# A new order of all steps, with the loads split and dealt anew to two queues, in a linear-attention and FFN kernel

## The chip, the cores and the metric

The kernel runs on one core of a Trainium2 chip. A core has five engines with an instruction queue each: TensorE (PE in the profile, with its weight loads as PEld), VectorE (DVE), ScalarE (ACT), GpSimd (POOL) and SyncE (SP). Each works through its queue in order. DMAs are issued by SP and ACT here, and moved by 16 DMA engines that both queues share. The metric is the device time of one execution in microseconds (us).

## The reference

Two branches read the same layer-normalized input, and the result is added to x. There is one batch of S = 2048 rows, width D = 448, H = 16 heads of 28, and F = 1792.

```python
xn = _layernorm(x)                                # no scale, no bias
# A: linear attention with a softmax feature map
q, k, v = split_heads(xn @ wqkv)
pq, pk = q @ w_phi, k @ w_phi                     # per head, 28 x 28
phi = lambda p: concat([softmax(p), softmax(-p)]) # 56 features a head
kv, z = phi(pk).T @ v, phi(pk).sum(rows)
o = (phi(pq) @ kv) / (phi(pq) @ z + 1e-6)
A = o @ wo
# B: FFN with Mish
h = xn @ w1 + b1
B = (h * tanh(softplus(h))) @ w2
return x + A + B
```

## The kernel before, in words

**An order written out by hand.** All work is cut into named steps. `ORDER` (L147) is a string of their names, and `run_order` calls them one after the other. Each step appends its instructions to the queues of the engines that it uses, and `Program.op` notes what each instruction reads and writes. `resolve` turns that into semaphore waits. So the string alone sets the order on each engine, and what waits for what follows from the data. Matmuls, evacuations and transposes go through helpers, so many steps share a line: L429 (`run`) issues the products of q, k, v and the first FFN layer, L509 and L511 (`evac`) copy PSUM to SBUF on ACT and DVE.

**Names of steps.** u is a pair of row tiles (0 to 7), t one tile (0 to 15). A final letter a, d, p, s or m names the engine (ACT, DVE, POOL, SP) or, for m, a DMA transpose issued by SP; b is a PE transpose evacuated by both ACT and DVE.

- `lx a.b`: load of x tiles a to b-1. `lkm`, `lvm`: rows 0 to 383 of the K and V weights; `lkt`: rows 384 to 447 of both, into each half of the partitions. `lp`: the 28 x 28 phi matrices in four small DMAs. `lqT0` to `lqT3`: the q weights by DMA transpose into `WqT`. `lb`: b1. `l1m`, `l1t`: W1's main and tail rows, `l2`: W2, `lo`: Wo.
- `pi`, `pw`, `pv`, `pp`, `pk`, `zero`: POOL writes constants (identity, zeros of Wbd, ones beside v, pads, mask, zeros for the products of `z`).
- `st t`: mean and variance of a tile (DVE: `BATCH_NORM_STATS2` at L466; ACT: two passes with a sum, L458 and L462). `rt`, `rs`: the reciprocal standard deviation of one or two tiles. `xn t`: normalize a tile; on ACT and POOL this first needs a shift that DVE computes (L486). `xt u`: transpose a normalized pair into `xnT`.
- `z12`: 12 products of zeros (L370). `wtk h`: PE transposes of the K weights into `WT`; `wmk h` and `wmq h`: fold phi into the K and Q weights (L571), results in `Wp[1]` (Wpk) and `Wp[0]` (Wpq). `qd` (DVE, L289) doubles columns of `WqT` and reads all four of its loads. `b1`: transpose of the bias.
- `k`, `q`, `v` with u and a part, `f q.fc` with a part: products of 64 weight rows at a time, which run in pairs on the two halves of the array. Parts A and B hold six matmuls each, H two (the tail rows). When the last part of a step is issued, its evacuation follows: two exponentials on ACT for k and q (L609, L682), one copy for v, one Mish on ACT for f (L703).
- `kn u.s`, `kc u`: normalize phi of the keys: sum and reciprocal on DVE, product on POOL (L621, L633). `kv u`: accumulate phi(k)ᵀv (L650), eight steps into one pair of banks; `kvz` evacuates it and SP transposes it into `KVZ`.
- `e t`: DMA transpose of phi(q) of a tile. `nd t`: numerator and denominator of a tile (PE at L723, then seven DVE instructions). `ot u`: transpose of the result. `wo u` with a part (L845) and `g t` (L828): the output projection and the second FFN layer, which accumulate into one bank per tile; the last of the four adds x on DVE (L793). `sto`, `stt`: stores.

**What sets the waits.** PSUM has eight banks, used as four pairs. `take2` gives a step the pair that has been idle longest in the order; a step's first product waits until that pair's last evacuation is done. A part of a step waits for the data named in its list `r`, before the change for all rows of its weight, tails included.

Of the kernel before, what the change touches and what calls it, by code (L numbers as in the profile page):

```python
# [5 lines left out]
ACT = mybir.ActivationFunctionType  # L6
# [6 lines left out]
D = 448  # L13
H = 16
# [136 lines left out]
st13d xn6d l1ts st15d xn7d xt3m v0Ha wmq1a wmq0a k2A rt12p rt13p xn13p xn12p st10d xt6m xn8p st14d k1A v1Bd k1B st11d  # L151
q2B k1H rs5p v1Ad q1H q2H v1Hd rt14a q1B xn10d q2A xn9d xn14d rt15p pk xt4m q0A q1A q0B k3B xn15d xt7m v6Ba k3H q0H
v6Aa xn11p kn0.1 k6H v6Ha k3A kn0.0 xt5m kn1.1 l1ms k6A v3Ad kc3 k6B v3Hd k7A v3Bd k7H v4Hd kn6.0 e3 v4Ad k7B v4Bd k4B
v7Ba k4H k4A e2 k5B kn7.1 v7Aa kn7.0 q4H k5A v7Ha kc2 e0 k5H q4A e5 f0.0B q4B f0.0H v5Bd f0.0A e9 f0.8H f0.8A v5Ad
kn5.0 f0.3B f0.8B v5Hd f0.3A e1 f0.4B f0.3H e8 q3B f0.4A f0.5A f0.4H f0.5H f0.2H f0.2A kn1.0 f0.5B kn4.1 q5H e4 q5A
f0.2B q3H kn6.1 loa q7B q5B q7A q7H kn5.1 kn4.0 kv2 kv6 ep kv1 kv0 kv5 kv7 kv4 kv3 q3A f1.0B kvz f0.9A e10 f1.0A f1.0H
e14 f0.9H e15 f0.6A f0.9B f0.7B f0.6H nd0 f0.7A f0.6B f0.11H f0.11A f0.7H f0.10B nd3 f0.11B f0.12A f0.10A e11 e6
f0.10H nd1 f0.12H e7 ot0m f0.1B f0.12B f0.1A f0.1H q6A q6H f1.13H nd2 q6B f1.5A f1.13A f1.4A f1.13B f1.5H f1.1H f1.1A
f1.4B f1.1B f1.5B f1.6A f1.6H e12 f1.4H ot1m f1.11A f1.6B f1.11B nd4 f1.12H f1.11H l2s f1.12A f0.13B f1.12B f1.7A nd5
f1.7H f0.13H f0.13A f1.2H f1.7B ot2m f1.2A nd7 wo0H f1.2B wo1B wo0A wo1A nd6 ot3m wo1H wo0B nd10 g2 g7 g3 g1 g0 nd12  # L160
e13 f1.10A f1.10H f1.9A f1.9H wo3B f1.10B nd13 f1.9B wo3A wo3H f1.8B ot6m f1.3H nd11 f1.3A ot5m g6 g5 f1.8H nd15 f1.8A
wo2H f1.3B sto1 wo2B nd14 nd9 wo2A nd8 g4 sto3 g14 g9 sto2 g12 ot7m g8 ot4m g13 wo7H wo4B wo7A wo5A wo6A wo5H wo6H
wo4A wob wo5B wo4H wo6B wo7B sto0 g10 g11 g15 sto6 stt14 sto5 sto4 stt15
"""
# [7 lines left out]
def _kernel(es, nc, A_x, A_wqkv, A_w_phi, A_wo, B_w1, B_b1, B_w2, out):  # L172
# [421 lines left out]

    def tok_works(u, W):
        return lambda b: [(bank(b + par)[:, 0:D],
                           lambda c, k, par=par: xnT[k[0]:k[1], u, xchunk(c, par), :],
                           lambda c, k: W[k[0]:k[1], c, :]) for par in range(2)]

    def v_mm(u, part, eng):  # L600
# [3 lines left out]
        pair_part(f"v{u}", part, tok_works(u, Wv), [("xnT", u), ("xnU", u)] + rows_of("Wv"), then)  # L604

    def k_mm(u, part):
        def then(b):
            for s in range(2):
                op("ACT", lambda e, s=s: e.activation(E_of(u)[:, s, :, :], two(b, D), ACT.Exp,  # L609
                                                      scale=1.0 if s == 0 else -1.0),  # L610
                   r=[pb(b), pb(b + 1)], w=[("E", u, s)], tag=f"exk{u}.{s}")
        pair_part(f"k{u}", part, tok_works(u, Wp[1]), [("xnT", u), ("xnU", u)] + [("Wp", 1, h, c) for h in range(2) for c in range(2)], then)

# [78 lines left out]

# [6 lines left out]
    def ffn1(q, fc, part):  # L699
        def then(b):  # L700
# [99 lines left out]
    def last_columns(t, b):  # L800
# [3 lines left out]
        def f(e):  # L804
# [6 lines left out]
            return ins  # L811
        pe(f, [("WoB",), ("W2",), ("oT", t // 2)] + [("act", fc, t // 8) for fc in range(FC)] + [("Wo", n) for n in range(4)],
           [pb(b)], f"l{t}")
# [166 lines left out]
```

## Time and profile before

| | |
|---|---|
| median of 3 runs | 154.04 us (153.67 to 154.15) |
| the profiled execution | 153.96 us, span 152.2 us |
| PE busy | 144.6 us (95%) |
| DVE busy | 101.1 us (66%) |
| ACT busy | 75.7 us (50%) |
| POOL busy | 44.3 us (29%) |
| chain that ended last | PE 78%, ACT 12%, DMA 4%, DVE 3% |

The span runs from the first to the last instruction; the execution's own time is 1.76 us longer. Shares of busy time are averages over the whole span. The chain is followed back from the last instruction, at each step to what released it.

### The profile page before, as it was taken

The numbers are of one execution on the slowest core, as the hardware profiler recorded it, in microseconds if no ns is written. First come the engines' busy times: TensorE is split into PE (matmuls) and PEld (weight loads), VectorE is DVE, ScalarE is ACT, GpSimd is POOL, SyncE is SP. The second block draws the span as 40 slices with busy tenths as digits, with TensorE's granted clock in tenths as the row PEclk, the third lists the DMA queues.
The fourth block names the chain that finished last, engine by engine and source line by source line (L and its number), as shares of the span: only waits on it lengthen the run. The fifth ranks groups of instructions, "written<-read, shape, count | busy, mean of one in ns | idle before, by whom it ended". The sixth has DMA issues, their size and how long they took to land.

```text
span 152.2 us, 3611 instructions
## 1 busy us (share of the span) xinstructions
PE 144.6 (95%) x1541; PEld 76.1 (50%) x1541; DVE 101.1 (66%) x223; ACT 75.7 (50%) x90; POOL 44.3 (29%) x65
## 2 busy tenths in 40 slices
PE   3978999989999979999999999999999999999993
PEld 1454545445444574445344455554544554559552
DVE  0699989599969903599606999535995999200721
ACT  3485999995995699778997730000500400000000
POOL 3385688969999950000000000000000000000000
PEclk9999999999999999999999999999999999999999
DMA  5995964989967243994399260500035000540204
GB/s 123 288 260 147 174 143 93 131 268 262 101 137 138 76 139 73 180 197 41 60 149 321 86 65 14 119 0 0 2 65 151 30 4 0 121 121 4 87 4 151
DMA packets 40436, 17.22 MB, mean 113 GB/s; under 512 B 34020, under 2 KB 39908, under 8 KB 40420
## 3 DMA queue, kind: packets, MB, share of 16 engines
q1 hardware_dynamic: 37548, 14.46, 46.9%
q10 hardware_dynamic: 2872, 2.53, 5.6%
q8 instruction: 12, 0.20, 0.5%
q14 instruction: 4, 0.03, 0.1%
HBM read 7.02 MB, written 1.84 MB: 58 GB/s over the span
## 4 chain that ended last, share of the span: by engine, by line
PE 78%; ACT 12%; DMA 4%; DVE 3%; issue 1%; ACTq 0%
PE PS L429 38%; PE PS L828 28%; PE PS L845 7%; DMA x_all<-in_A_x_dram 4%; ACT actT L609 3%; PE PS L723 2%; PE PS L650 2%; ACT actT L682 2%; ACT v_all L509 2%; DVE Sk L627 1%; ACT Wpq L509 1%; ACT Eq L682 1%; DVE v_all L511 1%; ACT Eq L509 1%; ACT Wpk L509 1%
## 5 line engine op out<-in xcount | busy, mean ns | idle before, releaser
L703 ACT ACTIVATE actT<-PS,b1T 128x1024 bf16<-128x1024 f32 x28 | 30.2, 1112 | 33.1 <-PE PS L429 33.0
L429 PE MATMUL PS<-xnT,W 64*128 64x512 bf16 x392 | 46.2, 376 | 0.0
L828 PE MATMUL PS<-W,actT 128*128 128x448 bf16 (+1 forms) x224 | 42.7, 351 | 0.0
L828 PEld LDWEIGHTS PS<-W,actT 128*128 128x128 bf16 x224 | 21.5, 98 | 20.3 <-issue 0.7
L429 PEld LDWEIGHTS PS<-xnT,W 64*128 64x128 bf16 x392 | 18.1, 94 | 21.0 <-ACT actT L703 0.4
L793 DVE TENSOR_TENSOR x_all<-PS,x_all 128x448 bf16<-128x448 f32 (+1 forms) x16 | 9.5, 616 | 20.3 <-PE PS L845 10.3
L621 POOL TENSOR_TENSOR actT<-actT,rSk 128x896 bf16<-128x896 bf16 x12 | 20.0, 1699 | 0.0
L609 ACT ACTIVATE actT<-PS 128x896 bf16<-128x896 f32 x16 | 13.7, 950 | 3.7 <-DVE stats L466 1.8
L429 PE MATMUL PS<-Wkv,xnT 64*128 64x448 bf16 x112 | 13.6, 349 | 0.6 <-DVE v_all L511 0.6
L429 PE MATMUL PS<-Wpk,xnT 64*128 64x448 bf16 x112 | 13.3, 349 | 0.5 <-ACT Wpk L509 0.5
L429 PE MATMUL PS<-Wpq,xnT 64*128 64x448 bf16 x112 | 12.7, 350 | 0.0
L466 DVE BATCH_NORM_STATS2 stats<-x_all 128x6 f32<-128x448 bf16 x15 | 9.2, 614 | 5.2 <-DMA x_all<-in_A_x_dram 5.2
L617 DVE TENSOR_REDUCE Sk<-actT 128x32 f32<-128x896 bf16 x12 | 12.5, 1043 | 0.0
L738 DVE COPY Sq<-PS 128x16 f32<-128x16 f32 x32 | 4.0, 167 | 12.5 <-PE PS L723 12.2
L749 DVE TENSOR_TENSOR xn<-v_all,rden 128x448 bf16<-128x448 f32 x16 | 10.0, 625 | 1.3 <-DMA Wkv<-xn 0.8
L746 DVE TENSOR_TENSOR v_all<-v_all 128x464 f32<-128x464 f32 x16 | 10.3, 642 | 0.6
L742 DVE TENSOR_TENSOR v_all<-PS,Sq 128x464 f32<-128x464 f32 x16 | 10.3, 642 | 0.5
L744 DVE TENSOR_TENSOR v_all<-PS,Sq 128x464 f32<-128x464 f32 x16 | 10.1, 630 | 0.0
L429 PEld LDWEIGHTS PS<-Wkv,xnT 64*128 64x128 bf16 x112 | 5.4, 94 | 6.0 <-DVE v_all L511 1.0
L682 ACT ACTIVATE actT<-PS 128x896 bf16<-128x896 f32 x10 | 8.4, 926 | 0.0
L429 PEld LDWEIGHTS PS<-Wpk,xnT 64*128 64x128 bf16 x112 | 5.3, 94 | 5.5 <-ACT Wpk L509 0.6
L429 PEld LDWEIGHTS PS<-Wpq,xnT 64*128 64x128 bf16 x112 | 5.1, 94 | 5.4 <-ACT actT L609 0.5
(85 smaller groups left out, 137.7 us busy)
## 6 DMA issues: line engine op xcount, KB each, us to landing
W<-in_B_w_dram SPq DMA_DIRECT2D x1, 1568.0 KB, 8.0
out_dram<-x_all SPq DMA_DIRECT2D x7, 224.0 KB, 2.2
W<-in_B_w_dram SPq DMA_DIRECT2D x1, 1344.0 KB, 7.2
x_all<-in_A_x_dram ACTq DMA_DIRECT2D x5, 224.0 KB, 4.1
Wo<-in_A_wo_dram ACTq DMA_DIRECT2D x2, 336.0 KB, 3.6
x_all<-in_A_x_dram SPq DMA_DIRECT2D x2, 224.0 KB, 4.9
W<-in_B_w_dram SPq DMA_DIRECT2D x2, 224.0 KB, 4.0
Wkv<-in_A_wqkv_dram SPq DMA_DIRECT2D x1, 336.0 KB, 4.2
```

Of the source, the lines that this page charges most:

```text
L429: ins = e.matmul(o, lhs(c, k), rhs(c, k), start=first and n == at[par][0], stop=last and n == at[par][-1])
L609: op("ACT", lambda e, s=s: e.activation(E_of(u)[:, s, :, :], two(b, D), ACT.Exp, scale=1.0 if s == 0 else -1.0), r=[pb(b), pb(b + 1)], w=[ ...
L617: op("DVE", lambda e: e.tensor_reduce(Sk[u][:, s, :], Eh(), AX.X, ALU.add), r=[("E", u, s)], w=[("Sk", u, s)], tag=f"Sk{u}.{s}")
L621: op("POOL", lambda e: e.tensor_tensor(Eh(), Eh(), ap_on(rSk[u][:, s, 0:1], [[1, 2 * H], [0, DH]]), ALU.mult), r=[("E", u, s), ("rSk", u, ...
L682: op("ACT", lambda e, s=s: e.activation(Eq_of(u)[:, :, s, :].rearrange("p i (h n) -> p i h n", n=64)[:, :, :, 0:QP], two(b, D).rearrange(" ...
L703: op("ACT", lambda e: e.activation(actT[:, q, fc, :], bank(b, 2), ACT.Mish, bias=b1T[:, fc:fc + 1]), r=[("b1T",), pb(b), pb(b + 1)], w=[(" ...
L742: op("DVE", lambda e: e.tensor_tensor(tv(t1[i]), num(0), sx(1), ALU.mult), r=[pb(b), pb(b + 1), ("Sq", i, 1)], w=[("t1", i)], tag=f"ta{t}")
L744: op("DVE", lambda e: e.tensor_tensor(tv(t2), num(1), sx(0), ALU.mult), r=[pb(b), pb(b + 1), ("Sq", i, 0)], w=[("t2",)], tag=f"tb{t}")
L746: op("DVE", lambda e: e.tensor_tensor(t1[i], t1[i], t2, ALU.add), r=[("t1", i), ("t2",)], w=[("t1", i)], tag=f"tc{t}")
L749: op("DVE", lambda e: e.tensor_tensor(o_sb[(t // 2) % 2][:, t % 2, :].rearrange("p (h d) -> p h d", d=DH), t1[i][:, :, 0:DH], ap_on(rden[i ...
L828: ins = e.matmul(bank(b)[:, 0:width(t)], act_of(fc, t), W2[:, fc, 0:width(t)], start=first and fc == 0, stop=last and fc == FC - 1)
L845: ins = e.matmul(bank(b)[:, 0:w], oT_of(u)[lo:hi, cc * P:(cc + 1) * P], Wo[lo:hi, cc, 0:w], start=first and n == at[par][0], stop=last and ...
```

## The change

The order is written anew from the first step to the last. With it:

- Loads. SP: x0-1, tail of Wv, b1, phi, Wv, x6-7, x8-11, the four WqT transposes, then x12-13 and W1's first and third part between the transposes of x. ACT: x4-5, x2-3, Wk, tail of Wk and Wv (to partitions 0 to 63 only; 64 to 127 get Wv's alone), x14-15, W1's second part. The tail of Wk is transposed from 64 rows and doubled in the evacuation (`doubled`).
- W1's main rows come in three loads, W2 in four (two issued by each of SP and ACT), Wo by SP.
- A part waits only for the rows that it reads: A and B for the main rows, H for the tails (`rows_of`, `folded`, `turned`).
- `y5.1` and `z10`: 11 products of zeros instead of 12, with `zero` ahead of `pi` on POOL.
- `wtk0` and `wtk1` are evacuated by ACT and DVE together, `wmk0` by ACT instead of DVE, `wmq1` by DVE instead of ACT. v2 and v7 go to DVE, v3, v4 and v5 to ACT. Statistics: tiles 1 and 10 on ACT, 5 on DVE.
- The first products are v0 and v2 (k0 and k2 before). The order of keys on DVE and POOL, of the f, nd and g steps, and of the stores is new too.
- Functions for early products on centred x (`center`, `center_T`, `minus_rstd`, `v_early`, `k_early`, `q_early`) are added; no step of the order calls them.

```diff
 ORDER = """
-pi lx1.2a pw table lx0.1s lx4.6a lx2.4a zero st1d lpa st5a st0d st4d st2d rs0p lvma rs2p lx6.8a xn0a xn1d lkms xn5p
-lkts xn4p lx8.10s lbs st3d z12 wtk0a rt2a wtk1d xt0b lqT3 rt3a wmk0d wmk1a pp b1 xt2b xn2d st8d lqT1 lqT2 lqT0 xn3d
-st9d k0B lx12.14a k2B xt1m st7d qd lx10.12s lx14.16a rt8p pv st6d k0A k0H st12d rt9p k2H v2Ba v0Ba v2Ha v2Aa v0Aa rs3p
...
+lx0.2s lx4.6a pw lvts zero st0d y5.1 lx2.4a pi lbs st4d pv rt4p table lkma lkta lps st1a rs0a st5d lvms xn0a rt5a xn1d
+xn4p st2d xn5p rt2a lx6.8s z10 b1 st3d xt0b rt3p wtk0b wtk1b xt2b wmk0a xn2d wmk1a lx8.12s xn3d v0Ba st6d st7d lqT0
+v2Bd st11d lqT2 v0Aa lx14.16a lqT3 st10a k2A rs3p st8d v0Ha k2H v2Hd lqT1 k0H xn6d rs5p xt1m qd v2Ad k2B k0B st9d
+wmq1d wmq0a k0A xn7d k1A k1H rt8p rt9p q0A xn9d lx12.14s pp xn8p k1B st15d xn10p q0H q1H q1A st14d st12d l1c0s q0B
+st13d xn11d xt3m v1Ad q2H q1B rs6p v1Hd xt4m pk q2A v1Bd q2B k4A v3Ba l1c2s k4H xt5m v4Ba v3Aa xn13d rs7a v3Ha k4B
+xn12d v4Aa k5H xn14d v5Ba xn15p xt6m k5B v4Ha v5Ha k5A kn1.1 k6B v6Ha v5Aa k6A v6Ba xt7m e2 e3 l1c1a kn1.0 k6H k7H
+kn4.0 k7A v7Hd kn4.1 kn2.0 kn2.1 v7Ad v6Aa k7B kc6 k3B v7Bd l1ts k3A k3H q4B f0.0B l2p0a q4H q4A f0.3A f0.0A f0.6B
+f0.0H f0.7B e9 kc3 f0.6H e1 f0.6A f0.3H e8 f0.7H f0.7A e0 f0.8A f0.8H e5 f0.4A f0.3B f0.4H f0.8B e4 q7H kn7.0 f0.4B
+q3H q7A q5A q3B kn7.1 q5B q7B f0.2B ep q5H kn0.1 q3A f0.2A kv4 l2p2s kn0.0 kv2 los kv3 kn5.1 kv0 kv1 kv6 kv7 kn5.0 wob
+kv5 f0.1A e15 kvz f0.2H f1.4B f0.1B e6 f1.8B f0.1H f0.5B f1.8H f1.8A f1.9A f1.9H e7 f0.5A f0.5H f1.9B f1.3B f1.4H
...
+wo4A wo3B ot7m wo5B wo3H wo7H wo7A wo4H sto2 wo5A wo4B wo3A wo7B g10 sto3 g9 stt14 g15 sto5 sto4 sto6 stt15
 """
...
+    def load_w1(c, eng):
+        dma(eng, lambda e: e.dma_start(W1[:, c, :], B_w1[c * P:(c + 1) * P, :]), w=[("W1m", c)], tag=f"ldW1m{c}")
...
+    def load_kv_tail(i, eng):
+        lo, hi = HALF[i]
+        dst, src = (Wv, A_wqkv[384:448, 2 * D:3 * D]) if i else (Wkv, A_wqkv[384:448, D:3 * D])
+        dma(eng, lambda e: e.dma_start(dst[lo:hi, 3, :], src), w=[("Wt", i)], tag=f"ldWt{i}")
...
-    def rows_of(name):
-        return [(name, 0), ("Wt", 0), ("Wt", 1)] if name in ("Wk", "Wv") else [(name, i) for i in range(3)]
+    def rows_of(name, part):
+        if name == "Wv":
+            return [("Wt", 0), ("Wt", 1)] if part == "H" else [("Wv", 0)]
+        return [("W1", 1), ("W1", 2)] if part == "H" else [("W1m", i) for i in range(3)]
+
+    def folded(which, part):
+        cs = (3,) if part == "H" else range(3)
+        return [("Wp", 1, c // 2, c % 2) if which else ("Wp", 0, c) for c in cs]
+
+    def turned(u, part):
+        return [("xnU", u)] if part == "H" else [("xnT", u), ("xnU", u)]
...
-    def load_w2(eng):
-        dma(eng, lambda e: e.dma_start(W2[:], B_w2.rearrange("(c p) d -> p c d", p=P)), w=[("W2",)], tag="ldW2")
+    W2_PARTS = ((0, 4), (4, 8), (8, 11), (11, 14))
+
+    def load_w2(n, eng):
+        a, b = W2_PARTS[n]
+        dma(eng, lambda e: e.dma_start(W2[:, a:b, :], B_w2[a * P:b * P, :].rearrange("(c p) d -> p c d", p=P)),
+            w=[("W2", n)], tag=f"ldW2p{n}")
...
+                    n = 64 if h and c else P
+                    ins = e.transpose(oT(c)[:, g, 0:n], Wk[0:n, 2 * h + c, g * GP:(g + 1) * GP], ident[0:n, 0:n])
...
+        def doubled(c):
+            to, at = WT[h][:, c], oT(c)
+            if not (h and c):
+                return to, at
+            return to.rearrange("p g (x n) -> p g x n", x=2), ap_on(at, [[P, G], [0, 2], [1, 64]])
...
+    for i in range(8):
+        for n in range(1, 5):
+            add(f"y{i}.{n}", warm, n)
```

More of the change, by code (lines that the diff above doesn't have):

```diff
@@ L153 @@
[L153 to L162, printed above, removed]
@@ new lines, in minus_rstd, with sign_rstd, v_early, then @@
+    def minus_rstd(u):
+        op("DVE", lambda e: e.tensor_scalar(nrstd[:, 2 * u:2 * u + 2], rstd[:, 2 * u:2 * u + 2], -1.0, 0.0, op0=ALU.mult, op1=ALU.add),
+           r=[("rstd", 2 * u), ("rstd", 2 * u + 1)], w=[("nr", u)], tag=f"nr{u}")
+    def sign_rstd(t, s):
+        return nrstd[:, t:t + 1] if s else rstd[:, t:t + 1]
+    def v_early(u, part, eng):
+        def then(b):
+            for i in range(2):
+                t = 2 * u + i
+                dst, src = v_all[:, u, i, :, 0:DH], bank(b + i)[:, 0:D].rearrange("p (h d) -> p h d", d=DH)
+                r, w = [pb(b + i), ("rstd", t)], [("v", u)] if i else [("vh", u)]
+                if eng == "ACT":
+                    op("ACT", lambda e, dst=dst, src=src, t=t: e.mul(dst, src, rstd[:, t:t + 1]), r=r, w=w, tag=f"vs{u}.{i}")
+                else:
+                    op("DVE", lambda e, dst=dst, src=src, t=t: e.tensor_scalar(dst, src, rstd[:, t:t + 1], 0.0, op0=ALU.mult,
+                                                                               op1=ALU.add), r=r, w=w, tag=f"vs{u}.{i}")
+        pair_part(f"v{u}", part, tok_works(u, Wv, True), x_res(u, part) + rows_of("Wv", part), then)
@@ new lines, in k_early, with then @@
+    def k_early(u, part):
+        def then(b):
+            for s in range(2):
+                for i in range(2):
+                    t = 2 * u + i
+                    op("ACT", lambda e, s=s, i=i, t=t: e.activation(E_of(u)[:, s, i, :], bank(b + i)[:, 0:D], ACT.Exp,
+                                                                    scale=sign_rstd(t, s)),
+                       r=[pb(b + i), ("rstd", t), ("nr", u)], w=[("E", u, s)] if i else [("Eh", u, s)], tag=f"exkc{u}.{s}.{i}")
+        pair_part(f"k{u}", part, tok_works(u, Wp[1], True),
+                  x_res(u, part) + folded(1, part), then)
@@ new lines, in q_early, with then @@
+    def q_early(u, part):
+        def then(b):
+            for s in range(2):
+                for i in range(2):
+                    t = 2 * u + i
+                    op("ACT", lambda e, s=s, i=i, t=t: e.activation(
+                        Eq_of(u)[:, i, s, :].rearrange("p (h n) -> p h n", n=64)[:, :, 0:QP],
+                        bank(b + i)[:, 0:D].rearrange("p (h n) -> p h n", n=QP), ACT.Exp, scale=sign_rstd(t, s)),
+                       r=[pb(b + i), ("Eqp", u % 3), ("rstd", t), ("nr", u)], w=[("Eq", u % 3, s)],
+                       tag=f"exqc{u}.{s}.{i}")
+        pair_part(f"q{u}", part, tok_works(u, Wp[0], True), x_res(u, part) + folded(0, part), then)
@@ L603, in then @@
                  [pb(b), pb(b + 1)], [("v", u)], f"ve{u}")
-        pair_part(f"v{u}", part, tok_works(u, Wv), [("xnT", u), ("xnU", u)] + rows_of("Wv"), then)
+        pair_part(f"v{u}", part, tok_works(u, Wv), turned(u, part) + rows_of("Wv", part), then)
     def k_mm(u, part):
@@ L611, in then @@
                    r=[pb(b), pb(b + 1)], w=[("E", u, s)], tag=f"exk{u}.{s}")
-        pair_part(f"k{u}", part, tok_works(u, Wp[1]), [("xnT", u), ("xnU", u)] + [("Wp", 1, h, c) for h in range(2) for c in range(2)], then)
+        pair_part(f"k{u}", part, tok_works(u, Wp[1]), turned(u, part) + folded(1, part), then)
     def k_norm(u, s):
@@ L685, in then @@
                    r=[pb(b), pb(b + 1), ("Eqp", u % 3)], w=[("Eq", u % 3, s)], tag=f"exq{u}.{s}")
-        pair_part(f"q{u}", part, tok_works(u, Wp[0]), [("xnT", u), ("xnU", u)] + [("Wp", 0, c) for c in range(4)], then)
+        pair_part(f"q{u}", part, tok_works(u, Wp[0]), turned(u, part) + folded(0, part), then)
     def q_turn(t):
@@ L705, in ffn1 @@
         pair_part(f"f{q}.{fc}", part, feat_works(W1, slice(fc * P, (fc + 1) * P), q, P),
-                  rows_of("W1") + [(n, u) for u in range(4 * q, 4 * q + 4) for n in ("xnT", "xnU")], then)
+                  rows_of("W1", part) + [x for u in range(4 * q, 4 * q + 4) for x in turned(u, part)], then)
     def act_of(fc, t):
@@ L811, in f @@
             return ins
[L812 removed]
+        pe(f, [("WoB",), ("oT", t // 2)] + [("W2", n) for n in range(4)] + [("act", fc, t // 8) for fc in range(FC)] + [("Wo", n) for n in range(4)],
            [pb(b)], f"l{t}")
@@ L830, in f @@
             return ins
-        pe(f, [("W2",)] + [("act", fc, t // 8) for fc in range(FC)], [pb(b)], f"g{t}")
+        pe(f, [("W2", n) for n in range(4)] + [("act", fc, t // 8) for fc in range(FC)], [pb(b)], f"g{t}")
         if last:
@@ L903, in _kernel @@
                 add(f"f{q}.{fc}{part}", ffn1, q, fc, part)
+    for u in range(4):
+        add(f"nr{u}", minus_rstd, u)
+        for eng, c in (("ACT", "a"), ("DVE", "d"), ("both", "b")):
+            add(f"ct{u}{c}", center_T, u, eng)
+        for part in "ABH":
+            add(f"v{u}{part}e", v_early, u, part, "ACT")
+            add(f"v{u}{part}f", v_early, u, part, "DVE")
+            add(f"k{u}{part}c", k_early, u, part)
+            add(f"q{u}{part}c", q_early, u, part)
+        for t in (2 * u, 2 * u + 1):
+            add(f"xc{t}d", center, t, "DVE")
+            add(f"xc{t}p", center, t, "POOL")
     add("kvz", kvz)
```

72 lines of the change are left out of this document (55 added, 17 removed).

## The prediction

> **What bounds the kernel now.** I read the page first, then the busy time by stretches, cut where the chain of waits changes engine, then that chain, then what TensorE waited for.
>
> ```profile
> span 152.2 us, 3611 instructions
> 11.92:16.10 4.18, 4.18 (x46) 2.16 (x48) 4.04 (x14) 2.05 (x3) 2.00 (x6) 1.00 0.92 145
> 16.10:34.20 18.10, 17.51 (x190) 9.02 (x186) 15.46 (x36) 17.73 (x25) 15.50 (x26) 1.00 0.81 167
> 34.20:52.94 18.74, 18.73 (x187) 8.86 (x189) 17.19 (x25) 13.78 (x15) 18.62 (x12) 1.00 0.76 139
> 52.94:57.17 4.23, 3.45 (x130) 3.22 (x132) 0.44 (x1) 4.02 (x5) 2.36 (x4) 1.00 0.49 155
> 57.17:91.00 33.83, 33.83 (x445) 16.22 (x446) 22.19 (x54) 27.28 (x26) 0.04 (x1) 1.00 0.68 132
> 91.00:149.25 58.25, 58.25 (x485) 31.77 (x484) 34.16 (x76) 4.24 (x4) 0.00 (x0) 1.00 0.20 52
> PE PS L429 <- DVE v_all L511: 0.6, 1, 0.6
> ```
>
> The second column of a stretch is its length, the third TensorE's busy time. From 11.92 to 149.25 TensorE works 135.96 of 137.33 us. It idles 0.59 in 16.1 to 34.2 (behind a DVE evacuation of v, as the last row says), and 0.78 inside the kv products (its row stands below). So a new order can win only three things: an earlier start than 11.92, the 0.59, the 0.78. It can lose by making TensorE wait anywhere. This is what sets 11.92:
>
> ```profile
> 1.74 5.48 DMA x_all<-in_A_x_dram
> 7.25 0.64 DVE stats L466
> 8.17 0.76 ACT xn L495
> 11.06 0.81 ACT Wpk L509
> 11.92 4.17 PE PS L429 x42
> ```
>
> Tiles 2 and 3 of x land at 7.23. Their statistics (st2) stand on DVE ahead of the shift that normalizing tile 0 needs, so tile 0 is done only at 8.93 (8.17 and 0.76), the K fold (Wpk) at 11.87, and k0B, the first bulk product, needs that fold.
>
> **The start.** Durations for the new path:
>
> ```profile
> 2.00:4.00 2.00, 1.70 (x5) 0.60 (x6) 0.37 (x1) 0.54 (x1) 0.25 (x2) 1.00 0.98 258
> 4.00:6.00 2.00, 2.00 (x6) 0.74 (x5) 1.72 (x5) 0.58 (x2) 0.62 (x2) 1.00 1.08 332
> 2.31 5.03 PE L370 MATMUL PS<-zeros 128*128 128x512 bf16 x12 [2.31 <-POOL zeros L322]
> 3.63 0.63 DVE L466 BATCH_NORM_STATS2 stats<-x_all 128x6 f32<-128x448 bf16 x1 [3.63 <-DMA x_all<-in_A_x_dram]
> 5.42 0.58 ACT L458 ACTIVATE junk<-x_all 128x448 bf16<-128x448 bf16 x1 [2.87 <-DMA x_all<-in_A_x_dram]
> 6.92 0.19 ACT L462 ACTIVATION_READ_ACCUMULATOR junk<-x_all,rmean 128x1 f32 x1
> 8.06 0.58 DVE L492 TENSOR_SCALAR xn<-x_all,mv,rstd 128x64 bf16<-128x64 bf16 x2
> 9.90 0.96 PE L571 MATMUL PS<-Wbd,Eq 112*128 112x112 bf16 x16 [0.34 <-ACT Eq L509]
> 11.51 0.16 DVE L511 CAST b1T<-PS 128x14 f32<-128x14 bf16 x1
> 11.59 0.41 DVE L511 COPY xnT<-PS 128x512 bf16<-128x512 bf16 x1
> 13.45 0.62 DVE L466 BATCH_NORM_STATS2 stats<-x_all 128x6 f32<-128x448 bf16 x1
> 14.20 0.59 DVE L466 BATCH_NORM_STATS2 stats<-x_all 128x6 f32<-128x448 bf16 x1
> ```
>
> In the new order x0-1 leads SP's queue and x4-5 ACT's; x2-3 is second on ACT's, and only then come Wk and Wv. Today 224 KB of x are in at 3.63. 448 KB need 0.8 us more at the 295 GB/s between the first two rows, at most 4.4; part of that was moving already, so I take 4.2 (ends 3.6, and 5.4, where the second pair landed). The wait for x2-3 goes, since 670 KB ahead of Wk land by about 5.4.
>
> What is late next is DVE itself, which never pauses from there: st0, st4, st5 at 0.75 (13.45 to 14.20) 2.25; shift 0.1; xn1 0.58; shift 0.1; st2 0.75; shift 0.1; b1 0.16; st3 0.75; its halves of xt0, wtk0 and wtk1 at 0.41 each 1.23. That is 6.0, so 10.2. ACT runs beside it and is sooner: st1 (5.42 to 7.11 for a tile today, 1.7), rstd 0.4, xn0 0.76, two more rstd, then 0.5 for each evacuation. The second half of the K fold is 8 of the 16 products of 0.96, 0.48, plus about 0.05 of signals: the bulk starts at 10.75. It starts with v0B, v2B, v0A, which need no fold, 1.7 us in which ACT evacuates both halves of it. The start gains 1.17 (ends 1.8 and -0.05).
>
> Zero products: `zeros` moves ahead of the identity on POOL, so 11 of them at 0.42 run from about 1.4 to 6.0 instead of 12 from 2.31 to 7.34. They hide under the loads, but TensorE then pauses until xt0 at about 7.35. The smaller transposes of wtk1 (64 rows) and wtk0/1 evacuated on both engines lie inside the sum above; they save under 0.2 us, and only off its path.
>
> **The middle.** ACT is the crowded engine there: it takes st10 (1.7) and one v evacuation more (five, not four), and v2 and the second Wpq half go to DVE. Its rows show room:
>
> ```profile
> 14.09 1.73 ACT L609 ACTIVATE actT<-PS 128x896 bf16<-128x896 f32 x2 [1.85 <-DVE stats L466]
> 35.75 1.73 ACT L609 ACTIVATE actT<-PS 128x896 bf16<-128x896 f32 x2 [1.51 <-PE PS L429]
> 37.83 0.92 ACT L509 ACTIVATE v_all<-PS 128x896 bf16<-128x896 f32 x1 [0.36 <-PE PS L429]
> 30.60 2.02 DVE L627 TENSOR_REDUCE Sk<-actT 128x64 f32<-128x1792 bf16 x1 [1.72 <-ACT actT L609]
> 33.12 1.03 DVE L511 CAST v_all<-PS 128x896 bf16<-128x896 f32 x1
> ```
>
> st10 fits into the 1.85 of idle ahead of the first exponentials, the added evacuation into the 1.51 and 0.36. I followed the four pairs of PSUM banks down the new order with 0.1 per matmul (4.17 for 42; an A or B part has 6, H 2), 1.73 for two exponentials, 0.9 to 1.0 for an evacuation (rows above): each pair is free before its next product, with as little as 0 to 0.4 us to spare (q0A at 18.1, k3B, f0.3A). The 0.59 goes: it came from v3's evacuation queued on DVE behind the long sum of k3 (last two rows); v3 moves to ACT, and k3 becomes the last of the keys.
>
> One wait is new. `qd` stands on DVE after st6, st7, st11, st8 and xn6 and needs all four WqT loads:
>
> ```profile
> 4.09 5.10 SPq L285 DMA_TRANSPOSE WqT<-in_A_wqkv_dram  x4
> DMA to landing us min/median/max: 3.7/4.6/5.4
> DMA to landing us min/median/max: 2.9/3.8/4.9
> DMA to landing us min/median/max: 2.8/3.3/7.7
> ```
>
> (Landing rows: WqT, xnT, EqT.) SP now issues the four phi loads, Wv, x6-7 and x8-11 first, about 5 us of issue, so the last WqT issue begins at 9.6 instead of 7.9 and lands at 13.3 to 15.0. DVE is at `qd` at 15.0, so I take no wait (end: 7.7 for the latency, +2.3). Behind `qd` come the evacuation of v2 (until 16.2) and of wmq1; wmq0 needs v2's banks while TensorE is there at 15.95: +0.25. xt4m and xt5m go out behind W1 loads on SP. xt4m is issued at 20.05 (xn8 on POOL, after `qd`'s followers on DVE) and lands 2.9 to 4.9 later, median 23.85; k4A is due at 23.9: 0, end +1.05.
>
> **kv, loads, tail.** The POOL must have normalized all keys before kv5:
>
> ```profile
> 45.03 9.99 POOL L621 TENSOR_TENSOR actT<-actT,rSk 128x896 bf16<-128x896 bf16 x6
> 56.88 0.29 PE L650 MATMUL PS<-actT,v_all 128*60 128x112 bf16 x4 [0.78 <-issue]
> q8 instruction: 12, 0.20, 0.5%
> W<-in_B_w_dram SPq DMA_DIRECT2D x1, 1344.0 KB, 7.2
> 65.89 0.26 DVE L738 COPY Sq<-PS 128x16 f32<-128x16 f32 x2
> 68.91 0.25 DVE L738 COPY Sq<-PS 128x16 f32<-128x16 f32 x2
> ```
>
> Sixteen halves at 1.67 (9.99 for 6) are 26.7 us. The first waits for rs7 on ACT (26.4 by the same walk), xn14 and a sum of 1.35 on DVE: 28.3 to 55.0. Ahead of kv stand 40.43 us of bulk products today (52.94 - 11.92 - 0.59), by count 1.8 more in the new order, so kv4 comes at 53.2 and kv5, seven steps of 0.41 later, at about 56.1: covered by 1 us, and if POOL is later, TensorE waits by as much. The 0.78 falls between two matmuls of one kv step, where no semaphore stands; the eight kv steps still follow each other without a break, so I leave it as it is (0 either way, ends -0.78 and +0.78). [...]
>
> W1 in three loads (two on SP, one on ACT at about 32) must be there for f0.0B at 37.8; 448 KB should take between the 4 us of 224 KB and 7.2: cost 0, cover 1 us. W2 in four is needed only by g3 at about 94: cost 0. The Wo loads leave ACT, which frees about a microsecond of ACT ahead of the second exponentials; TensorE didn't wait there. The nd steps, the Mish steps and the last three products (g10, g9, g15 for g10, g11, g15) keep counts and kinds. Walking the nd banks through DVE (3.0 each, 65.89 to 68.91) gives 0.1 to 0.4 of slack and no wait: 0, end +0.6. The helpers for early k, q, v, centring and negative rstd are in no step of the order and cost nothing.
>
> **Sum.** -1.17 - 0.59 + 0.25 = -1.51. The profiled execution took 153.96 (span 152.2 and 1.76 around it), 0.08 under the median of 154.04. So 152.45, say 152.5.
>
> **Rivals.**
> 1. *POOL bounds kv.* The keys are counted to 55.0, but every slip of DVE or ACT in 15 to 28 comes out there. 2 us of slip cost 1: 153.4. For it: POOL is busy 18.62 of 18.74 in 34.2 to 52.94. Against: what feeds it (ACT's exponentials, DVE's sums) has idle time today, as the rows of the middle show.
> 2. *TensorE falls back to half speed.* The zero products take 419 ns for 512 columns, twice a later one, for 5.03 us. If the pause from 6.0 to 7.35 undoes them, the fold runs 0.45 longer and some 2.3 us of bulk at half rate lose 1.15: 154.05. For it: release took 5.03 us of slow work today, and the new zero run is 4.6. Against: today's pause of 0.34 ahead of the fold harms nothing, the bulk then runs 42 matmuls in 4.17. The granted clock reads 1.00 even in 2 to 4 us, so only durations show it. [...]
> 3. *Slower: WqT late.* If the last WqT takes the longest latency seen, 7.7, it lands at 17.3. DVE stands at `qd` for 2.3 us with v2's banks, wmq1 and xn7 behind it, and TensorE with it: 154.75. It decides from 15.0; at 16.5 the gain is gone.
> 4. *It does little*: xt4m, xt5m and the nd banks each wait, +1.05 and more: 153.7.
>
> **How the numbers follow.** Forecast 0.58 (own range 151.4 to 153.2), rival 1 0.12, rival 2 0.12, rival 3 0.10, rival 4 0.08. A measurement tells 0.3%, 0.46 us, from nothing. Faster takes the forecast and most of rival 1: 0.68. Same takes rivals 2 and 4, mostly: 0.19. Slower is rival 3 and a tail of rival 2: 0.13. The range 151.2 to 154.2 reaches from an early start without the kv pause to rivals 1, 2 and 4, and leaves out rival 3 and the ends.
>
> **What would show it.** Right: the first bulk product is v_all's (Wkv) at about 10.75; DVE without a gap from 4.2; no wait of TensorE on L511-like evacuations over 0.3 us before 52; the pause in kv still there. Wrong: first statistics after 5; `qd` after 15.5; 448-column pairs over 0.2 us after 10.75; kv waiting for POOL.

## The result, and the profile after

The changed kernel took 151.82 us (median of 4 runs: 151.08, 152.49, 152.88, 151.16) against 154.09 of the kernel before, run beside it (153.67 to 154.29, 4 runs): a ratio of 0.9864, with a 95% interval of 0.982 to 0.9908. The forecast was 152.5. The four runs stand in two groups, 151.1 and 152.5 to 152.9, and the experiments must explain both. (Ratios leave out runs over 1.5% above the fastest of a kernel, so they can differ a little from the ratio of the medians.)

The profiled execution is the fastest of the four: 151.08, with a span of 149.4 and 1.7 around it. The head of its page:

```profile
span 149.4 us, 3636 instructions
PE 144.1 (96%) x1540; PEld 78.2 (52%) x1540; DVE 99.3 (67%) x223; ACT 78.5 (53%) x98; POOL 41.3 (28%) x59
```

Busy time by stretches, cut as before (length, then TensorE's busy time, its weight loads', VectorE's, ScalarE's, POOL's; the granted clock stands third from the end):

```profile
0.00:10.75 10.75, 7.96 (x60) 4.27 (x62) 6.33 (x22) 7.14 (x18) 5.15 (x18) 1.00 0.92 242
10.75:16.00 5.25, 5.25 (x61) 2.77 (x60) 5.11 (x14) 4.69 (x10) 2.73 (x6) 1.00 0.91 206
16.00:34.20 18.20, 18.20 (x198) 10.64 (x196) 16.01 (x37) 17.62 (x24) 12.65 (x21) 1.00 0.72 142
34.20:52.94 18.74, 18.74 (x195) 10.30 (x192) 14.96 (x22) 17.03 (x19) 18.59 (x12) 1.00 0.84 185
52.94:57.17 4.23, 4.23 (x138) 3.50 (x133) 1.12 (x2) 4.19 (x6) 2.20 (x4) 1.00 0.81 175
57.17:91.00 33.83, 33.82 (x430) 16.22 (x426) 21.46 (x54) 25.99 (x25) 0.00 (x0) 1.00 0.65 108
91.00:146.40 55.40, 55.40 (x475) 30.14 (x472) 33.57 (x75) 1.83 (x2) 0.00 (x0) 1.00 0.19 50
```

From 10.75 on, TensorE is busy in every stretch for its whole length. The 0.59 (16.1 to 34.2) and the 0.78 (52.94 to 57.17) are both gone. What TensorE waited for at all, all of it ahead of the bulk (in us: total, times, longest):

```profile
PE PS L404 <- POOL mhalf L359: 1.4, 1, 1.4
PE PS L805 <- DMA b_rows<-in_B_b_dram: 0.6, 1, 0.6
PE PS L538 <- ACT xn L529: 0.5, 1, 0.5
PE PS L538 <- POOL xn L532: 0.3, 1, 0.3
```

And the start of the chain of waits (start, length, what):

```profile
0.81 3.34 DMA x_all<-in_A_x_dram
4.17 0.64 DVE stats L500
...
7.94 0.15 DVE shift L520
8.09 0.09 DVE b1T L545
8.19 0.01 issue
8.19 1.05 POOL xn L532 x2
9.24 0.14 issue
9.38 0.55 PE PS L538 x7
9.93 0.79 PE PS L612 x16
10.72 4.84 PE PS L463 x50
```

The first statistics start at 4.17 and the bulk at 10.72, where before they were 3.63 and 11.92. The chain no longer goes through the load of x2-3 nor through the evacuation of the K fold.

Where the time went: the span fell by 2.8 (152.2 to 149.4). The start gave 1.20, the wait for v3 0.59, the pause in kv 0.78; together 2.57. The rest is less TensorE time between the start of the bulk and the end, 135.64 busy (the sum of the last six stretches) against 135.96; why the same products took 0.3 less stays open.

### The profile page after: what moved, and what is told of

The parts are those of the page before. It is cut to its first block, busy times and chain, and to the rows that moved or that the text cites. A ratio compares the mean times of both kernels' runs of the same rounds, so it can differ in the third digit from the quotient of the medians.

```text
span 149.4 us, 3636 instructions
## 1 busy us (share of the span) xinstructions
PE 144.1 (96%) x1540; PEld 78.2 (52%) x1540; DVE 99.3 (67%) x223; ACT 78.5 (53%) x98; POOL 41.3 (28%) x59
## 4 chain that ended last, share of the span: by engine, by line
PE 92%; DVE 3%; DMA 2%; POOL 1%; issue 0%
PE PS L463 50%; PE PS L938 28%; PE PS L955 7%; PE PS L833 2%; DMA x_all<-in_A_x_dram 2%; PE PS L760 2%; DVE stats L500 1%; PE PS L612 1%; POOL xn L532 1%; DVE mv L501 0%; DVE x_all L903 0%; PE PS L538 0%; DVE xn L526 0%; DVE shift L520 0%; DVE x_all L924 0%
## 5 line engine op out<-in xcount | busy, mean ns | idle before, releaser
L463 PE MATMUL PS<-xnT,W 64*128 64x512 bf16 x392 | 45.0, 376 | 0.0
L463 PEld LDWEIGHTS PS<-xnT,W 64*128 64x128 bf16 x392 | 19.2, 94 | 20.5 <-ACT actT L813 0.4
L500 DVE BATCH_NORM_STATS2 stats<-x_all 128x6 f32<-128x448 bf16 x14 | 8.5, 607 | 4.2 <-DMA x_all<-in_A_x_dram 4.2
L463 PEld LDWEIGHTS PS<-Wpq,xnT 64*128 64x128 bf16 x112 | 6.0, 94 | 4.7 <-DVE Wpq L545 0.3
L463 PEld LDWEIGHTS PS<-Wpk,xnT 64*128 64x128 bf16 x112 | 6.0, 94 | 4.4
L463 PEld LDWEIGHTS PS<-Wkv,xnT 64*128 64x128 bf16 x112 | 5.9, 94 | 4.5 <-ACT actT L792 0.2
```

The source lines that it names most:

```text
L463: ins = e.matmul(o, lhs(c, k), rhs(c, k), start=first and n == at[par][0], stop=last and n == at[par][-1])
L500: op("DVE", lambda e: e.bn_stats(stats[:, t, :], x_all[:, t, :]), r=[("x", t)], w=[("st", t)], tag=f"bn{t}")
```

## The experiments

They ask four things: why the same kernel gives two times; what took the kv pause away; which part of the start gained; what the loads did. They ran in three groups, each on one chip beside the kernel before, whose median was 153.89 in the first (the first four kernels below, without the repeat of 16 zero products), 153.77 in the second (the three edits of the kernel before, and the bursts) and 153.81 in the third (the repeat with 16 zero products and the two that build on it).

### The changed kernel again

No edit.

> The changed kernel once more, to see how its executions spread beside the next two. Theory W (the clock's release decides): the four executions seen fall into two groups, 151.1 and 152.5 to 152.9, and the slower group is one in which the 11 products of zeros end before the clock is released, so the spread of 1.4 to 1.8 us comes back here. Theory N (ordinary noise): values fill the space between 151.0 and 152.9 without groups.

Measured: 152.6 (152.28 to 153.59, 6 runs), ratio 0.9919 (0.989 to 0.9949). None of the six came near 151.1. In five of them the mean granted clock is 0.989, as in the run of 152.88 above. This profiled execution (152.74, span 151.0) shows where the clock went; two stretches of it (the clock stands third from the end):

```profile
5.85:9.27 3.42, 1.97 (x26) 1.46 (x24) 3.32 (x14) 2.92 (x11) 2.38 (x5) 1.00 1.12 314
9.27:12.68 3.41, 3.12 (x30) 2.51 (x31) 2.96 (x10) 2.64 (x5) 0.94 (x3) 0.50 0.91 143
```

By the trace's clock record the full clock came at 5.85, was halved at 9.27 and came back at 12.68; 0.5 x 3.41 of 151 us is the missing 0.011 of the mean. So the expectation had the spread right, but not how it comes about: the full clock came while the zeros still ran (to 6.14), and was halved 3.13 after their end. In the products it shows like this (start, length, how many); first this execution, then the 151.08 one:

```profile
10.29 1.70 PE L612 MATMUL PS<-Wbd,Eq 112*128 112x112 bf16 x16
11.92 2.23 PE L463 MATMUL PS<-Wkv,xnT 64*128 64x448 bf16 x18
```

```profile
9.77 0.95 PE L612 MATMUL PS<-Wbd,Eq 112*128 112x112 bf16 x16
10.65 1.88 PE L463 MATMUL PS<-Wkv,xnT 64*128 64x448 bf16 x18
```

The fold takes 1.70 instead of 0.95, the bulk starts 1.27 later, and its first 18 products take 0.35 more: together 1.62 of the 1.66 between the two executions. So the slower group is the forecast's rival 2, in part of the executions (one trace shows it, and for the others their mean clock).

### 16 zero products instead of 11

```diff
-... lx6.8s z10 b1 st3d ...
+... lx6.8s z15 b1 st3d ...
```

> 16 products of zeros instead of 11 (y5.1 and z15), so that TensorE works without a pause from 1.4 to at least 7.3 us, up to the first transposes. Theory W: every execution is released before the bulk starts, the slower group is gone, and the median is 151.1 (150.9 to 151.4). Theory N: the same spread as without the added products, median 151.8. A third possibility is that the added products delay the first transposes where the clock is released late (zeros until 8.2, xt0 0.7 us later): then a few tenths more, at most 151.9.

Measured: 151.64 (151.29 to 151.85, 5 runs), ratio 0.9847 (0.9821 to 0.9872); the interval doesn't meet that of the unaltered kernel on the same chip, and the mean clock was 1.0 in every run (the profiled one holds no clock record; there the fold's 0.95 shows the full speed). Run again in the third group:

> 16 products of zeros again, as the base of the next two: 151.3 to 151.9, without a slower group.

Measured: 151.55 (151.16 to 152.21, 6 runs), ratio 0.9851 (0.9827 to 0.9875), mean clock 1.0 in all. In the first of the two profiles the zeros reach up to the bias transpose at 7.17 (timeline):

```profile
1.42 5.81 PE L404 MATMUL PS<-zeros 128*128 128x512 bf16 x16 [1.42 <-POOL mhalf L359]
```

The same stretch in which TensorE was busy for 1.97 is busy for 3.05 (busy time by stretches):

```profile
5.85:9.27 3.42, 3.05 (x31) 1.86 (x28) 3.32 (x14) 2.93 (x10) 2.55 (x6) 1.00 1.12 306
```

With the longer run of zeros the slower group is gone: in none of the 22 executions with 16 zero products (the last two kernels below included) is the mean clock under 0.998, where 6 of the 10 with 11 have 0.989. The edit does two things, it fills most of the pause and it lengthens the run of zeros (5.81 against 4.71); no run parts them. This version beats both kernels in the median: 151.6 against 152.6 and 153.9 on one chip. It doesn't beat the changed kernel's best executions (151.08), nor reach the 151.1 expected. In its first profile TensorE waits for the DMA transpose of tiles 10 and 11 (`xt5m`), which took 3.6 us from issue to landing in the 151.08 execution, where TensorE doesn't wait for it:

```profile
PE PS L463 <- DMA xnT<-xn: 0.3, 1, 0.3
```

In the second profile this wait is not there. Why the transpose is late in the first stays open.

### One zero product

```diff
-... rt2a lx6.8s z10 b1 st3d ...
+... rt2a lx6.8s b1 st3d ...
```

> One product of zeros instead of 11. Theory W: TensorE reaches the first bulk product at half speed in every execution; the transposes and folds run 0.4 to 0.9 us longer and 2 to 3.4 us of bulk lose half, so 152.7 to 154.0, and the products of 448 columns in the profile after 10.7 us take about twice their time for some us. Theory N: no change, 151.8.

Measured: 153.17 (152.35 to 154.88, 12 runs), ratio 0.997 (0.9944 to 0.9996). In its profile (152.35) the transposes of the K weights run at half speed, 2.00 for 16, where the 151.08 execution has 1.15, and the bulk starts at 11.91:

```profile
8.21 2.00 PE L582 MATMUL PS<-ident,Wkv 128*112 128x128 bf16 x16
11.91 1.31 PE L463 MATMUL PS<-Wkv,xnT 64*128 64x448 bf16 x12
```

The fold, from 10.86, took 1.11 for 16, between the 0.95 of the 151.08 execution and the 1.70 at half clock, so the full speed came within it; in the 151.08 execution the clock record has it from 6.29. The bulk itself ran at full speed here, so of theory W the slow transposes and the time came out, but not the slow bulk; this profiled execution is the fastest of the twelve. In the median 15 more zero products are worth 1.5 (153.17 against 151.6), and 10 more 0.6 (against 152.6). With one, 0.7 is left of the 2.3 by which the version with 16 beats the kernel before.

### K's products first

```diff
-... xn3d v0Ba st6d st7d lqT0 v2Bd st11d lqT2 v0Aa lx14.16a ...
+... xn3d k2A  st6d st7d lqT0 k2B  st11d lqT2 k0B  lx14.16a ...
```

(v0Ba, v2Bd and v0Aa take the places of the three k parts.)

> The first products of the new order are k2A, k2B, k0B instead of v0B, v2B, v0A (three exchanges in the order, nothing else). Theory: the bulk then waits for the second half of the K fold on ACT (12.14 us in the profile of the changed kernel) and starts at about 12.2 instead of 10.7, so 1.4 to 1.5 us more, 152.6 in the faster group. Rival: DVE and ACT, not TensorE, set the pace of the stage after it, the later start is caught up by 20 us, and the time stays at 151.1.

Measured: 155.73 (153.58 to 157.62, 12 runs), ratio 1.0033 (0.9998 to 1.0067) without the six slowest. The wait that the v products cover is there, in the timeline of the profiled execution, the slowest (157.62):

```profile
13.77 3.79 PE L468 MATMUL PS<-Wpk,xnT 64*128 64x448 bf16 x18 [1.13 <-ACT Wpk L548]
```

Those 18 took 3.79 where 18 of the same shape took 1.88, and the next eight, from 17.36, took 1.21, where eight in the 151.08 execution take 0.94. So this execution pays the wait of 1.13, 1.9 more in these 18 products, and the half speed ahead of them (the fold takes 1.70 here too); its bulk starts 3.12 later than in the 151.08 execution. The wait alone did not keep the clock back: the transposes of the K weights, which stand ahead of it, already take 2.00 for 16 from 8.29, where the 151.08 execution has 1.15. The zeros end at 6.30, as there (6.31); why the full speed came so much later stays open.

Even the three fastest executions (153.58 to 153.70, mean clock 1.0) are 2.5 over 151.1, where 1.4 to 1.5 was expected. No trace shows them, so where the last 1.0 goes stays open. That v goes first is a part of the gain.

### The kernel before, its zero products cut small

Nearly the same columns of zeros (6160 and 6144), 56 more instructions on TensorE's queue (28 products of two instructions each) ahead of everything.

```diff
-            for _ in range(n):
-                ins = e.matmul(bank(b)[:, :], ... [[0, TCW]]) ...
+            for _ in range(40):
+                ins = e.matmul(bank(b)[:, 0:154], ... [[0, 154]]) ...
```

> The kernel before, with its 12 products of zeros of 512 columns cut into 40 of 154 columns: the same columns, 28 matmuls and 28 weight loads more on TensorE's queue, nothing else. [...] Theory D (the pause waits for data, such as the last normalized keys): it stays after the 124th matmul and the time is unchanged.

Measured: 153.36 (153.07 to 153.72, 12 runs), ratio 0.997 (0.9955 to 0.9984). The kv products run through:

```profile
52.51 3.33 PE L650 MATMUL PS<-actT,v_all 128*60 128x112 bf16 x128
```

No data, buffer or order of the kv steps was touched; only their place in the instruction stream. So the pause is not a wait for data. It did not move to another product either, it is gone; what TensorE waited for in it no run shows.

The median falls by 0.4 and not by 0.78. By the profile other waits take the rest: for v3's evacuation TensorE waits 0.68 here (0.59 before), and shortly behind kv for the exponentials of q:

```profile
PE PS L429 <- ACT actT L682: 0.3, 1, 0.3
```

(In this profile the start is 0.35 earlier as well, by an earlier landing of x2-3, which the edit doesn't touch.)

### The kernel before, with the statistics of tile 2 behind tile 1

```diff
-... st4d st2d rs0p lvma rs2p lx6.8a xn0a xn1d lkms ...
+... st4d rs0p lvma lx6.8a xn0a xn1d st2d rs2p lkms ...
```

> The kernel before, with the statistics of tile 2 (and the standard deviation after them) moved behind the normalization of tiles 0 and 1 on DVE; its loads stay as they are. Theory O (the order on DVE held tile 0 back): tile 0 is normalized about 1.0 us sooner (by 7.9 instead of 8.93), the bulk starts at about 11.0 and the time falls by 0.7 to 1.0, to 153.2. Theory L (the dealing of the loads is what buys the start): the start moves by less than 0.3 us, because the phi loads (in at 9.3) or the K weights set the fold.

Measured: 153.54 (153.18 to 153.93, 12 runs), ratio 0.9975 (0.9959 to 0.9991). The bulk starts at 11.17 instead of 11.92, so the order on VectorE alone gives 0.75 of the 1.2. In both profiles the statistics of tile 2 start at 7.25, as x2-3 lands, so the two can be compared. What is late next there are loads of phi and of the K weights, as TensorE's waits say:

```profile
PE PS L575 <- DMA Wbd<-in_A_w_phi_dram: 0.5, 1, 0.5
PE PS L551 <- DMA Wkv<-in_A_wqkv_dram: 0.4, 1, 0.4
```

The first bulk products and the last ones of kv in its timeline:

```profile
11.17 1.12 PE L433 MATMUL PS<-Wpk,xnT 64*128 64x448 bf16 x10 [0.40 <-ACT Wpk L513]
56.13 0.29 PE L654 MATMUL PS<-actT,v_all 128*60 128x112 bf16 x4 [0.78 <-issue]
```

The kv pause stays at the same product, 0.75 earlier in time, with the instruction stream as it was. Of the 0.75, the median shows only 0.2. In the old order the start hangs on the landing of x2-3: with the statistics of tile 2 at 6.90, 7.25 and 7.54 (the profile with zeros cut small, the one before, and the next one below) the bulk starts at 11.57, 11.92 and 12.21. So executions with an early landing have less to gain, 0.4 by an estimate from 11.57 and 11.17; whether that is all of it stays open.

### The kernel before, v3 evacuated by ScalarE

```diff
-... v3Ad kc3 k6B v3Hd k7A v3Bd ...
+... v3Aa kc3 k6B v3Ha k7A v3Ba ...
```

> The kernel before, with the evacuation of v3 on ACT instead of DVE. Theory: the wait of 0.59 us of TensorE at 33.6 goes, and if ACT has room for 0.9 us more the time falls by 0.4 to 0.6, to 153.5. Rival: ACT is full there, the exponentials come 0.9 us later, the wait appears at another pair of banks, and the time stays at 154.1 or grows.

Measured: 152.97 (152.54 to 153.56, 10 runs), ratio 0.9939 (0.9919 to 0.9958). The wait is gone, and 0.8 with it, more than the 0.59; a wait of 0.34 for POOL's keys comes up in kv:

```profile
55.19 1.24 PE L654 MATMUL PS<-actT,v_all 128*60 128x112 bf16 x32 [0.34 <-POOL actT L625]
```

The profile shows no idle at the old pause, though the products and weight loads ahead of it are as many and in the same order as before. By the starts of the products, 0.28 us still pass between the 124th and the 125th (0.99 in the kernel before, about 0.025 for most others): most of the pause seems to fall together with the wait ahead of it. From its first bulk product to the end of kv TensorE takes 44.15 where it took 45.18; 0.59 of these 1.03 are the wait for v3, about 0.2 the shorter kv, and where the rest went stays open.

### The changed kernel, W1 and W2 in one burst each

W1's three loads go out together on SP behind `xt7m`, W2's four on SP ahead of `e14`.

```diff
-... q1A st14d st12d l1c0s q0B ... k4A v3Ba l1c2s k4H ... xt7m e2 e3 l1c1a kn1.0 ...
+... q1A st14d st12d q0B ... k4A v3Ba k4H ... xt7m l1c0s l1c1s l1c2s e2 e3 kn1.0 ...
-... l2p0a ... l2p2s ... l2p3s ... l2p1a ...
+... f1.5H l2p0s l2p1s l2p2s l2p3s e14 ...
```

> The changed kernel with W1's three main loads issued by SP one behind the other after the last transpose of x, where the one load stood before, and W2's four loads one behind the other ahead of e14. Theory: W1 lands at about 36 to 37, as f0.0B needs it at 37.4, so TensorE waits 0 to 1 us there and the rest is as before: 151.1 to 152.1 in the faster group. Rival: the loads fill the queue ahead of the transposes of phi(q) (the kernel before had one such issue of 5.15 us), those come too late for q7 and q3, and it costs over 1 us.

Measured: 151.66 (151.4 to 154.35, 6 runs), ratio 0.9875 (0.9828 to 0.9922). Four of the six stand at 151.4 to 151.7, 0.3 to 0.6 over the 151.1 of the changed kernel's faster group (which ran on another chip). In the chain, the transposes of phi(q) now stand on SP's queue behind the burst (L805), and W1's tail rows behind them:

```profile
32.17 3.78 SPq L805
...
36.63 4.35 DMA W<-in_B_w_dram
...
41.03 11.94 PE PS L468 x114
```

The chain runs through the load of the tail rows, which it doesn't in the changed kernel, but TensorE loses little by it: kv starts at 52.90, against 52.66 in the 151.08 execution. W1's main rows were used at 37.45 without a wait. So splitting and dealing W1 and W2 is worth about half a microsecond, as far as times of two chips can be compared.

### 16 zero products, x2-3 behind the weights

```diff
-... y5.1 lx2.4a pi lbs st4d pv rt4p table lkma lkta lps ...
+... y5.1 pi lbs st4d pv rt4p table lkma lkta lx2.4a lps ...
```

> On the base with 16 products of zeros, the load of x2-3 goes behind those of the K weights and tails on ACT's queue, as late as the old dealing had it; the order on DVE stays. Theory O (what bought the start is that DVE normalizes tiles 0 and 1 ahead of the statistics of tile 2): x2-3 then lands at about 7.0 to 7.3, where DVE wants it at 7.15, so the start moves by 0 to 0.3 us and the time by as much, 151.5 to 152.0. Theory L (the early x2-3 bought it): the start goes back towards 11.9, 152.5 to 153.

Measured: 151.82 (151.63 to 152.07, 5 runs), ratio 0.9868 (0.9845 to 0.9891), against 151.55 for its base; the two intervals overlap, so the 0.27 between them is not clear of noise. VectorE waits for the load, and the bulk starts at 11.2 instead of 10.8:

```profile
7.77 0.63 DVE L505 BATCH_NORM_STATS2 stats<-x_all 128x6 f32<-128x448 bf16 x1 [0.51 <-DMA x_all<-in_A_x_dram]
```

### 16 zero products, a shorter start

The statistics of tile 3 go behind the evacuations of the K weights, the transpose of x2-3 behind `v0B`, and v0 and k0 ahead of v2 and k2.

```diff
-... z15 b1 st3d xt0b rt3p wtk0b wtk1b xt2b wmk0a xn2d wmk1a lx8.12s xn3d v0Ba st6d ...
+... z15 b1 xt0b wtk0b wtk1b st3d rt3p wmk0a xn2d wmk1a lx8.12s xn3d v0Ba xt2b st6d ...
-... v2Bd st11d lqT2 v0Aa lx14.16a lqT3 st10a k2A rs3p st8d v0Ha k2H ... k2B k0B ... wmq0a k0A ...
+... v0Aa st11d lqT2 v0Ha lx14.16a lqT3 st10a k0A rs3p st8d v2Bd k2H ... k2B k0B ... wmq0a k2A ...
```

> On the base with 16 products of zeros, the start is shortened where the profile of the changed kernel shows it held: the transposes of pair 2 and 3 (they wait for xn5 on POOL until 9.24) go behind v0B on TensorE, the statistics of tile 3 behind the evacuations of the K transposes on DVE, and v0 and k0 come ahead of v2 and k2. Theory: the folds end at about 10.0 and the bulk starts there instead of at 10.7; the time falls by 0.4 to 0.7, to 151.0. Rival: what follows (xt2, WqT, the first exponentials on ACT) isn't ready sooner, TensorE waits 0.5 us or more between 11 and 16, and the time stays at 151.6.

Measured: 152.44 (152.32 to 152.49, 6 runs), ratio 0.9906 (0.9888 to 0.9923): not the gain that was expected but 0.9 slower than its base. The bulk starts at 10.63, 0.2 sooner than in the base's profile (10.80), but the transposes of x2-3, which stood ahead of it, now stand in it. From there to the fold of the q weights it takes 5.49 instead of 4.84, and the fold 1.38 instead of 0.89. VectorE stands 0.85 for the deviation of tile 3, which POOL now computes late, and everything behind it on VectorE slips until TensorE waits for v2's evacuation between the two halves of the fold:

```profile
11.67 0.59 DVE L531 TENSOR_SCALAR xn<-x_all,mv,rstd 128x64 bf16<-128x64 bf16 x2 [0.85 <-POOL rstd L514]
17.00 0.57 PE L617 MATMUL PS<-Wbd,WqT 112*128 112x112 bf16 x8 [0.31 <-DVE v_all L550]
```

## Why the prediction was right, and which terms were off

The time came out 0.7 below the forecast and inside its own range. That it lies so near is in part luck: for an execution at full clock the sum is about 1.0 too high by two terms, and such executions (151.08 and 151.16) lie just below the own range's 151.4; the slower executions, which the sum left out, make up for it in the median. By its steps:

- **The start: right.** 10.75 was said, 10.72 measured; -1.17 against -1.20. The first statistics at 4.2 came at 4.17. The path was a shade different: VectorE does run without a gap and is through at 9.90, 0.3 sooner than said, but TensorE gets to the second half of the fold at 9.93, for it first transposes the other normalized pair, which comes from POOL at 9.24. With 16 zeros and the load of x2-3 late, 0.5 of wait on VectorE went with a start 0.4 later and 0.27 in the median, not clear of noise; so the new place of that load is a small part of the gain.
- **The wait for v3: right.** 0.59 was taken as gone, and it is gone. Undone alone in the kernel before it went with 0.8, but there the pause in kv shrank too.
- **The new wait at wmq0: the first mis-sized term, +0.25 said, 0 measured.** VectorE was to be at `qd` at 15.0. It was there at 14.33, didn't wait for the last WqT, and had v2 out by 15.6, when TensorE was still at `wmq1`, the first eight of these 16 products:

```profile
14.33 0.22 DVE L310 COPY WqT<-WqT 128x256 bf16<-128x256 bf16 x1
14.53 1.09 DVE L545 CAST v_all<-PS 128x896 bf16<-128x896 f32 x1
...
15.49 0.96 PE L612 MATMUL PS<-Wbd,WqT 112*128 112x112 bf16 x16
```

- **The pause in kv: the second, 0 said, -0.78 measured.** The prediction kept it because it stands between two matmuls of one step, where no semaphore is. That reasoning showed it was not data; it didn't show that it would stay. The three profiles with the old TensorE queue have it at the same product (in one shrunk behind a wait), whether the bulk starts sooner or later, and the small zero products take it away. In the new order, with 1009 instructions of TensorE ahead of kv against 969 by the traces, it is gone too. No run shows what it waits for. The prediction had given -0.78 as an end of the term, but its sign of being right, the pause still there, did not come true.
- **With both corrected** the sum is 152.45 - 0.25 - 0.78 = 151.42, against 151.08 for the profiled execution. The start and the lower TensorE time above make up the rest.
- **Rival 1 (POOL bounds kv): did not happen.** The last key was to be done at 55.0; it was done at 54.8, where POOL goes on to something else, and kv, from 52.66, ran through:

```profile
44.84 9.98 POOL L731 TENSOR_TENSOR actT<-actT,rSk 128x896 bf16<-128x896 bf16 x6
...
52.66 3.34 PE L760 MATMUL PS<-actT,v_all 128*60 128x112 bf16 x128
...
54.76 0.14 POOL L929 MEMSET WoB<- 64x64 bf16 x1
```

- **Rival 2 (half speed again): happens in part of the executions**, 1 of 4 and 5 of 6 by their mean clock of 0.989. The price was right as a sum (1.6 said, 1.62 in the profile of the repeat; 152.3 to 152.9 against 151.1), but not in its parts: the fold ran 0.75 longer where 0.45 was said, the bulk's first 18 products 0.35 where 1.15 was said, and 0.52 lay ahead of the fold (10.29 against 9.77). No run of this kernel shows the 2.3 us of bulk at half rate; the half clock in the repeat lasted 3.41 us, and only 0.76 of it lay behind the start of the bulk (11.92 to 12.68). The chance of 0.12 was low for what 6 of 10 executions did. The forecast's sum has nothing for the pause behind the zeros, and in the repeat the clock was halved after a stretch of 3.42 in which TensorE was busy for 1.97. The 151.08 execution had 2.05 of 3.41 from 6.29 on, where its full clock came, and kept it:

```profile
6.29:9.70 3.41, 2.05 (x31) 1.81 (x31) 3.34 (x14) 2.98 (x9) 2.58 (x6) 1.00 1.13 324
```

  The two differ by 0.08 of busy time, with matmul ends that are modelled, and no run shows what halved the clock in the one and not in the other. Nor is every execution explained: 152.49 and 153.59 have a mean clock of 1.0. A late full clock doesn't show in that mean (the kernel with one zero product has 1.000 too, and so has the 157.62 with K first), so it may be that, but no trace shows these two.
- **Rivals 3 and 4: no, in the profiled execution.** The last WqT landed at 12.67, before `qd`; no part of the nd steps, of xt4m or xt5m made TensorE wait. In the version with 16 zero products xt5m did, for 0.3. W1 was there in time with less to spare than the 1 us claimed: the last of its main rows, issued at 31.23, landed at 37.01 and was used at 37.44.

## What to carry to other kernels

Let a warm-up reach close to the first real product, as the 16 zero products do here (none of 22 executions had a mean clock under 0.998, where 6 of 10 with 11 had 0.989), and judge a kernel by many executions: one profile of the same kernel shows 151.08 at full clock, another 152.74 with 3.41 us at half clock. Before reordering, look for what stands ahead of the needed instruction on an in-order queue: one set of statistics moved behind the tile that was needed first gave 0.75 of the 1.2 us at the start. The pause of 0.78 that no semaphore explained stayed at one product while TensorE's queue stayed as it was (in one profile shrunk behind a wait), and was gone in every profile with another queue; don't count such a pause as fixed when you reorder, and don't count on all of it either, for in the old order only 0.4 of the 0.78 came out.

## What the runs showed of the hardware

- In the profile of the repeat the granted clock was 0.50 from 9.27 to 12.68 us and 1.00 again from there on; in the 3.42 us ahead of it TensorE was busy for 1.97. In the 151.08 execution it stayed at 1.00, with TensorE busy for 2.05 of the 3.41 us from 6.29 on. What decided between them is not shown.
- At half clock the fold of 16 products took 1.70, at full clock 0.95.
- With 11 zero products the full clock came at 6.29 in the 151.08 execution, and the 16 transposes of the K weights took 1.15; with one zero product they took 2.00, and the full speed came within the fold, from 10.86 on.
- With K first the slow products cost more than the wait ahead of them: 18 bulk products took 3.79 instead of 1.88, behind a wait of 1.13.
- The pause of 0.78 in a burst of 128 products of 25 ns went away when 56 instructions were put in front, some 45 us earlier: the 128 then ran through in 3.33.
- TensorE waited 0.3 for the DMA transpose `xt5m` in one profile with 16 zero products, and not at all in the other with the same loads, nor in the 151.08 execution, where it took 3.6 us from issue to landing.
